# Nystrom attention with a mixture-of-experts layer on one core: a new order of the same work

## The chip, the cores and the metric

The kernel runs on one core of one Trainium2 chip. The metric is the device time of one execution in microseconds; several executions of the same kernel are timed and their median is given. A profile is one execution of its own.

## The reference, cut to what matters

Eight batches with eight heads of 576 positions and 64 channels go through Nystrom attention with 32 landmarks; the result, seen as 4608 tokens of 512 channels, goes through a top-1 layer of eight experts (512 to 1024 to 512).

```python
q_lm = q.reshape(B, H, m, S // m, D).mean(axis=3)          # k_lm likewise
A, Bm, C = sm(q, k_lm), sm(q_lm, k_lm), sm(q_lm, k)        # softmax of scaled products
Z = Bm.transpose(0, 1, 3, 2) / (norm1(Bm) * norminf(Bm) + 1e-06)
for _ in range(6):
    Z = 2 * Z - Z @ Bm @ Z
x = (A @ Z @ C @ v).transpose(0, 2, 1, 3).reshape(B * S, H * D)
xn = x / (norm(x) + 1e-06); en = expert_emb / (norm(expert_emb) + 1e-06)
logits = xn @ en.T / tau; expert_idx = argmax(logits)
probs = softmax(logits); gate_w = probs[arange(N), expert_idx]
out = gate_w[:, None] * (relu(x @ w1[expert_idx]) @ w2[expert_idx])
```

## The kernel before

The kernel works batch by batch and guesses, for each of the eight batches, one expert for all of its tokens (`guess`, `choose`); the guess is compared with the exact choice per token at the end, and a general path, which this input does not take, mends tokens that were guessed wrongly. So one batch b of attention is followed by one pair of expert layers: `first(b)` (W1, 512 to 1024, line 1469) and `second(b)` (W2, line 1498). The attention product with V is not written out; the product of the 32-row middle matrix and W1 (`first_weights`, `scaled`) makes a small weight `ww`, with which `first` multiplies the transposed softmax `ab` of the queries. Both expert layers work on 16-bit halves: a number is a high and a low half, and three products stand for one.

For each batch the attention side does this. `loads` and `load_values` bring K, Q and V. `sums` (lines 676 and 679) adds up 18 positions per landmark, partly by a POOL addition of halves and then a DVE reduction, partly by DVE alone. `inverse` and `powers` (to line 1020) make the 32x32 softmax matrix and its iterated inverse in tiny 32-bit products, each answered by a copy (`ek`, line 1016 on ACT or 1018 on DVE) and a DVE addition (line 1020). `values`, `peak`, `shifted`, `turned`, `weighted` make C and its product with V. `queries` and `scored` make A transposed (`ae`, `am`, `asum`, `at`, `ab`, lines 927 to 951). `landmarks` joins them into the small matrix `wt`. `rows`, `route` and `gates` make the exact logits and gates. On the weight side `weights` loads W1 and W2 of the guessed expert in four quarters each (the guess is read as a register, `gi`, line 1174); `first_scale` takes the sum of squares of W1 (four ACT steps, line 1346), `second_weights` the sum of absolute values of W2 (line 1425 on ACT or 1427 on DVE) and its two halves (lines 1450 to 1454). `hidden` makes the two halves of a hidden tile `ht` (ACT, line 1462, then DVE, line 1464, which frees the PSUM bank); `outputs` scales a chunk of results (line 1554 on DVE or 1556 on ACT) and sends it out.

All of these are Python generators that ask for one thing at a time: an operation on an engine, one of two engines for a movable copy (`"any"`), or a buffer or bank (`"get"`). The class `Weave` (line 165) holds them, and nothing in it decides anything: four tables written out in the file do. `TURNS` (line 56) is the sequence of generators to step, two base-36 digits for each, 2,705 steps in all. `CHOICES` (line 107) says for each movable copy which of its two engines takes it. `BANKS` (line 111) gives the first PSUM bank of each allocation. `WARM` (line 115) says before which turn how many units of 128 columns of idle products `keep_warm` (line 595) issues on PE, in matmuls of up to 512 columns into a bank that nobody reads. Each engine executes its instructions in the order in which the turns issue them, so the order across the engines is that of the table, held together by semaphores.

```python
            elif ask[1] == "pe":
                if turn in WARM:
                    warm(WARM[turn])
            self._step(n, got)
```

Of the kernel before, what the change touches and what calls it, by code (L numbers as in the profile page):

```python
# [53 lines left out]
BUFS = dict(k=2, q=2, v=2, ek=4, u=3, ec=2, ct=2, ae=3, at=2, st1=4, st2=4, w2=6, ww=2, ht=12, ab=3, yt=3, land=3, wt=3)  # L54

TURNS = (
    "060000060600330b000633060b330706073c0c3c0108000836000035013601013600013g0c013h0c34343g0101343j013h3401010c0134"
    "0134013k340101013734370134013m013f010i3o0h3j3o3j1i3m3l3o1j3f1i3n3o3o3j3n3m3o3m3f3o3k1i3o3n3o3j3o3l3k3k3o3k3o3i"
    "3n3f3m3o3l3o3n3o3o3o3o1i3o3i3m3o3l3m3f3o3f1k3o1i3n020h3m3s3o021i021k1i1i3m3m1k383838021l3n1l3n1k411j413n1k3n1k"
    "3r3m1k1k411j1k0d411l3m1k020d2n1k453n0e1l3m420e021j421j451j3q4247472m3q023n1j432m2m02384100451m4338383q38492m3n"  # L60
    "3q021j3q3s493s2m2m2m4a1m383q0i024a0i1m4e2m2m2m3q024c4c023q3q4i4d024d1m0n020n4g4j024e2m382m4h021m4f2m021m2m2m2m"
    "4g1m4f1m1n4t02382m4t4r2m1m024u4s021m2m1m2m4h38024s4i1m4u1m4i1m1n4w4w4v1m4y4i1n1o4y4i4y2m4y2m0i1m4x2m4r1n4v4x4z"
    "4z1m1m500o1m4y1m4f39391m2n1m50524f511n1m2n1m0t1n2n395251392n2n0o2n513t3t1p2m2n544y4y551p1o4y5557542n51551o0o0t"
    "572n3a1r1o4y2n533a3a1p2n532n0o532n2n1r4b533a1o4y552n2n3a2n2n5i3a2n3b553b543b3b3b2n1n2n4y1o2n2n5i2n4y555k1o2n5i"
    "1o2n555k1n5k2n5i5k5k031r5k035k1r03034b55034y032n2n2n2n034j2n035k5k2n544b4y031r032n035k4y4y551r2n1p1p5k034j4j4j"
# [24 lines left out]
    "05282bb805299v2v05050505052v052vao2vao052v052b0529282v2vap2v2b2vap9v0505052b2v2905b8ao2905059v052v2929bb2abb9i"  # L90
    "9v2b9ubbbabbbbbbbb29ba2b2v2v9u29akagb02vbcbdbd2v2b2va8ag4q2b2bbd2v2v2b2v2v2vbbbcbe2bbebc5fbb7v2vbb2vbb7v2b7v2b"
    "2vbb7vbbbf7vbb2v2v2w2bbb7w7w7w2w2v7w2bbb2v2v2vbbbfbbbe2v2v2vbb2v7w2b2b2bagagbb9k2b7ubhbhbhbbbi2bag9kbbbb1dbj9l"
    "2b9l9l2b2w2w2x2wbg1dbibj9lbm2wbl2wbi9lbibjbm9lblbp2w2wb1bjbq2wbp2wbpbrbp7xbgbp9l2wbr9lbubo2w2wbo3x1ebubu2w2xbu"
    "2xbubububsbvbt2w1e2wbt7x2wbs5f2wbybz2b2w2wbi2d2d7xbzbqc12dbi2w3b2wbi2wbjc27x2xbw2xbv2c2c2c2dc32d2dbw7x2cc37xc0"
    "c4c0c4c4c42xc2c12xb1byc4bic4b12x2xc6c7c7bi2xc4c4bic4c42xc82x2c2c2c2xbic62x2x2xbjbjcac82gc5bfc8cacacac5ca2x2x2g"
    "2cc4c82dc8b29lb22ebjc5c5c5bj2x9l9l2xc92xce2x2ebj9lbi2xc52x2e2g2x7xcecccbcbcbbib3cccc2x2ecb2x9mbj2dccb32xc93xb3"
    "b3cb2x2xbj2x2xb3ce9m2xb39m6hbj2g2x2g9m6h6hcj2g2e2e9n2g2xci2gci2g9n2e9n2e2e6hcj2g2x9ncj2x2g2x2x2ecjcj2g9n2g2xci"
    "b34q2g9n2f2gcbba9ob32x2g2x9lcncn2g2x2x2xcb2x9o2x2x2e9ockcn2gclclclcm9o2x2y2x2ycncc2ycccockcmcccn2y2ycp9ocpcm2y"
    "6h2y2gcn2y2y2y2y4qcucncrcr2i2i2z9o2y2ycc2yctcqcw2hcu2y2gctco2y2ycq2gcxcc2ycv2hcw2y2y2gb32y2hd0cv2h2zcc2y2gcy2i"
    "d22zcccx2ycbcycbd22hck2hc9csczd0d12y9oczd32gd42zd5d12zb32jcsd52h2hd42z4q2icsd39o2j2j2z2z2z2j2j5f2jcs2icb2z2z2z"  # L100
    "cb2zcb2i2z2l2z2l2z2z2z2z2z2l2zb32i2i2l2l2zcscscscs2l2j2jcs9icbcs2k2z2j2jcs2z2z2z2z2j2z2z2z2zdeda7x2z2z2z2zdade"
    "cccc2l2zdd2z2l2l2zdcdddd2zde7rda2zdcdcdbb32l2l2l30302zb42z2z2z2z2l2l2ldgb42zdg2zdf2l2l2zdfdfb42z2l2l2l2z3030b4"
    "b47x3030di302l3030dbdi30dmdkdbdmdldj3x2l30303030dk30dndo31do30302l303x30dpdldjdpdq3130dqdr30dn302l3030dvdt3131"
    "31dvds31dudrdudtdsdw31dw31317x31b53131313131b5b5b5b53131b6co3131b631b631b631b631dz31dh31b6b6b6b69odhdh31313131"
    "dzdzdz31319odzdz31313131dz31dz31dzb6dzdz32e031313131dx3131dydx31b031313132b3dydy3132e1e031dx3131e13131e03132e2"
    "e231313131e1e3e2e3e3")
CHOICES = (
    "01110100000001001010010010000000000000000000000010010010101000001010001101001001000001000110011101001110000000"
    "00000001000110000111110110001000000100100000000100110001000000000000001011001101001010101100100110010001001011"
    "010100100011111010100001100110")  # L110
BANKS = (
    "05150606460234605105507521370123476057614071230371567154135125251750567065467012417260450475047547107127024056"
    "75075074501651234761532604541316412371273101560510601504764750127501765212301276004465045710267106725430156035"
    "67301605017604750756730152654136712510042005705406575075654601234076521340762617156721340632061734074023")
# [50 lines left out]
class Weave:  # L165
# [55 lines left out]
    def run(self, turns, choices, banks, warm):  # L221
        choices, banks = iter(choices), iter(banks)
        for turn, n in enumerate(turns):
# [15 lines left out]
                if len(ask) > 6:  # L239
# [1414 lines left out]
```

## Time and profile before

| | us |
|---|---|
| median of 3 runs | 416.08 |
| lowest, highest of the runs | 413.51, 417.13 |
| the profiled execution | 416.43 |
| its span, first to last instruction | 414.7 |
| PE busy in the span | 393.4 |
| DVE busy | 338.0 |
| ACT busy | 237.2 |
| POOL busy | 77.8 |

The span is what the views of the profile are in; what lies around it (416.43 against 414.7) belongs to the launch. PE is the matrix engine, DVE the vector engine, ACT the scalar engine, POOL the general one, SP the engine that issues most DMAs. PE's busy time is modelled from pipelined products, so a busy PE is not PE at its peak.

### The profile page before, as it was taken

To read this page: it belongs to the slowest core of one execution; us is meant where nothing else is said; L and a number is where in the kernel's file an instruction comes from. 1 tells how busy PE (TensorE), PEld (TensorE's weight loads), DVE (VectorE), ACT (ScalarE), POOL (GpSimd) and SP (SyncE) were. 2 spreads that over 40 slices of the span, in tenths; PEclk is the share of its full clock that TensorE was granted. 3 is DMA by queue.
4 is the path that set the end of the run, shared out by engine and by line. 5 is a ranking of instruction groups with operands and counts; after the bars stand their busy time and mean duration, and the time that the engine had idled before them with its cause. 6 is when DMAs were issued, how large, how long until landed. Compare 5 with 4: busy or idle time off the path is not lost.

```text
span 414.7 us, 14529 instructions
## 1 busy us (share of the span) xinstructions
PE 393.4 (95%) x6078; PEld 242.3 (58%) x6078; DVE 338.0 (81%) x989; ACT 237.2 (57%) x530; POOL 77.8 (19%) x82
## 2 busy tenths in 40 slices
PE   4978999999999999999999998999999999999994
PEld 1445754577655774556755575456755585467644
DVE  5789998998798999968898899867899888777421
ACT  1267993475579757535748478635539657436310
POOL 5142146201220233202321241100302210000100
PEclk9699999999999999999999999999999999999999
DMA  8795793355596798052679067310492129231031
GB/s 312 298 363 240 275 351 127 118 189 192 159 380 220 240 320 310 36 195 71 237 269 382 32 172 308 115 36 17 130 339 103 63 57 346 114 133 39 3 140 60
DMA packets 23946, 77.68 MB, mean 187 GB/s; under 512 B 3008, under 2 KB 6336, under 8 KB 22080
## 3 DMA queue, kind: packets, MB, share of 16 engines
q1 hardware_dynamic: 23584, 76.49, 51.4%
q8 instruction: 49, 0.80, 0.8%
q10 hardware_dynamic: 288, 0.18, 0.2%
q14 instruction: 25, 0.20, 0.2%
HBM read 61.92 MB, written 14.75 MB: 185 GB/s over the span
## 4 chain that ended last, share of the span: by engine, by line
PE 62%; DVE 26%; ACT 5%; issue 3%; POOL 1%; DMA 1%; ACTq 0%; DVEq 0%
PE ps L513 60%; DVE ht L1464 4%; DVE w2c L1454 4%; DVE ksum L679 2%; DVE qsum L679 2%; POOL half L676 1%; DVE ae L927 1%; PE ps L599 1%; DVE ww L1411 1%; ACT ht L1462 1%; ACT junk L1217 1%; DVE asum L940 1%; DVE am L934 1%; DMA k_t<-kT 1%; ACT w2c L1452 1%
## 5 line engine op out<-in xcount | busy, mean ns | idle before, releaser
L513 PE MATMUL ps<-w2c,ht 128*128 128x512 f16 (+2 forms) x1176 | 197.2, 340 | 0.0
L513 PEld LDWEIGHTS <-ht 128*128 128x128 f16 (+1 forms) x1176 | 94.9, 102 | 81.0 <-issue 2.3
L513 PE MATMUL ps<-ab,ww 128*128 128x288 f16 x768 | 101.0, 286 | 1.9 <-DVE ht L1464 1.3
L513 PEld LDWEIGHTS <-ww 128*128 128x128 f16 x768 | 73.6, 98 | 26.0 <-issue 5.6
L1462 ACT ACTIVATE ht<-ps 128x288 f16<-128x288 f32 x128 | 47.4, 412 | 35.9 <-PE ps L513 35.3
L1464 DVE SCALAR_TENSOR_TENSOR ht<-ps,ht 128x288 f16<-128x288 f32 x128 | 54.0, 444 | 10.2 <-ACT ht L1462 9.6
L1454 DVE SCALAR_TENSOR_TENSOR w2c<-wstage,wsc,w2c 128x1024 f16<-128x1024 f32 x32 | 42.9, 1341 | 1.0 <-ACT w2c L1452 0.9
L1346 ACT ACTIVATE junk<-wstage 128x1024 bf16<-128x1024 f32 x32 | 33.9, 1060 | 0.7 <-DMA wstage<-w 0.3
L1217 ACT ACTIVATE junk<-ps 128x512 bf16<-128x512 f32 (+1 forms) x40 | 23.9, 596 | 15.0 <-DVE lg L1211 6.7
L1235 POOL TENSOR_TENSOR nrm<-ssq,half 128x5 f32<-128x5 f32 x8 | 10.3, 1283 | 111.3 <-ACT junk L1217 111.3
L1452 ACT ACTIVATE w2c<-wstage,wsc 128x1024 f16<-128x1024 f32 x23 | 26.2, 1148 | 6.5 <-DVE wsc L1436 6.3
L1556 ACT ACTIVATE yt<-ps,gfac 128x512 f32<-128x512 f32 (+1 forms) x24 | 15.0, 631 | 21.3 <-PE ps L513 15.8
L676 POOL TENSOR_TENSOR half<-q_t 128x576 f32<-128x576 f32 x13 | 17.9, 1376 | 46.2 <-DVE ksum L679 16.0
L961 POOL TENSOR_TENSOR ae<-ae,asum 128x576 f32<-128x576 f32 x13 | 15.2, 1166 | 59.0 <-DVE wgd L1118 19.0
L961 POOL TENSOR_TENSOR ae<-ae,am 128x576 f32<-128x576 f32 x14 | 16.6, 1192 | 42.6 <-DVE am L934 38.6
L676 POOL TENSOR_TENSOR half<-k_t 128x576 f32<-128x576 f32 x11 | 14.2, 1295 | 54.7 <-DMA k_t<-kT 24.6
L1411 DVE SCALAR_TENSOR_TENSOR ww<-ps,wsc,ww 128x1024 f16<-128x1024 f32 (+1 forms) x18 | 20.4, 1157 | 0.6 <-ACT ww L1409 0.6
L1409 ACT ACTIVATE ww<-ps,wsc 128x1024 f16<-128x1024 f32 (+1 forms) x18 | 17.5, 1016 | 5.7 <-PE ps L513 3.2
L1425 ACT ACTIVATE junk<-wstage 128x1024 bf16<-128x1024 f32 x18 | 18.9, 1050 | 0.2
L829 ACT ACTIVATE ec<-ps,cneg 128x576 f32<-128x576 f32 x16 | 11.8, 739 | 9.8 <-DVE cneg L823 7.5
L513 PE MATMUL ps<-ek 32*32 32x64 f32 (+1 forms) x768 | 16.0, 214 | 0.9 <-DVE ek L1020 0.7
L513 PEld LDWEIGHTS ps<-ek 32*32 32x32 f32 x768 | 11.5, 105 | 9.0 <-issue 4.2
(216 smaller groups left out, 528.2 us busy)
## 6 DMA issues: line engine op xcount, KB each, us to landing
wstage<-w SPq DMA_DIRECT2D x64, 512.0 KB, 6.7
v<-v SPq DMA_DIRECT2D x16, 512.0 KB, 5.3
k_t<-kT SPq DMA_DIRECT2D x7, 1152.0 KB, 7.9
q_t<-qT SPq DMA_DIRECT2D x7, 1152.0 KB, 7.1
out<-yt SPq DMA_DIRECT2D x31, 256.0 KB, 3.3
abs__137<-ab SPq DMA_DIRECT2D x8, 576.0 KB, 5.2
k_t<-kT SPq DMA_DIRECT2D x2, 576.0 KB, 4.3
q_t<-qT SPq DMA_DIRECT2D x2, 576.0 KB, 6.7
```

The lines of the kernel that those rows point to most:

```text
L513: pe.matmul(o, lhsT, rhs, start=start, stop=stop)
L676: pool.tensor_tensor(out=half, in0=sv[:, :, :, 0:9], in1=sv[:, :, :, 9:18], op=ALU.add)
L961: pool.tensor_tensor(out=x, in0=x, in1=z, op=op)
L1217: act.activation(junk[lo:hi, 0:512].rearrange("p (j g x) -> p j g x", j=4, g=2), pfv[lo:hi, :, n, :, 0:D], AF.Square, accum_out=ssq[lo:hi, ...
L1346: act.activation(junk, stage[1, b, q], AF.Square, accum_out=sq[:, q:q + 1])
L1409: act.activation(ww[:, 0], pw, AF.Copy, scale=sc)
L1411: vec.scalar_tensor_tensor(out=ww[:, 1], in0=pw, scalar=sc, in1=ww[:, 0], op0=ALU.mult, op1=ALU.subtract)
L1425: act.activation(junk, stage[2, b, q], AF.Abs, accum_out=sq[:, q:q + 1])
L1452: act.activation(w[:, 0], st, AF.Copy, scale=sc)
L1454: vec.scalar_tensor_tensor(out=w[:, 1], in0=st, scalar=sc, in1=w[:, 0], op0=ALU.mult, op1=ALU.subtract)
L1462: act.activation(ht[:, 0, r], ph[:, 0:HS], AF.Relu)
L1464: vec.scalar_tensor_tensor(out=ht[:, 1, r], in0=ph[:, 0:HS], scalar=0.0, in1=ht[:, 0, r], op0=ALU.max, op1=ALU.subtract)
```

## The change

All four tables are replaced; no other line differs. `TURNS` has the same 2,705 steps in another order. `CHOICES` moves copies: of the absolute sums of W2, ACT has 24 of 32 instead of 18; of the output scalings, 31 of 41 instead of 24; of the transposed scores' copies of 512 columns, 10 of 16 instead of 14; of the inverse's copies, 12 of 25 instead of 15; of the W2 halves, 24 of 32 instead of 23. POOL has 28 of 32 subtractions and multiplications of A instead of 27; its halves of the landmark sums stay at 24. `BANKS` gives other banks. `WARM` has twelve entries as before, 194 units in place of 153.

```diff
 TURNS = (
-    "060000060600330b000633060b330706073c0c3c0108000836000035013601013600013g0c013h0c34343g0101343j013h3401010c0134"
+    "060006060b0000060607063300330b3334340037000136070008010801003701010137353h01010c35013g35353h01013g01353j013i35"
...
 CHOICES = (
-    "01110100000001001010010010000000000000000000000010010010101000001010001101001001000001000110011101001110000000"
+    "01111000000011011100010000000000000000000000000000010100010000010000001010000001000110100000111010101110000000"
...
-WARM = {20: 38, 49: 19, 51: 6, 63: 5, 76: 2, 96: 12, 113: 8, 129: 17, 150: 17, 194: 20, 204: 2, 214: 7}
+WARM = {21: 77, 44: 20, 59: 4, 87: 8, 97: 12, 115: 8, 124: 7, 131: 19, 138: 1, 147: 18, 181: 18, 207: 2}
```

PE at the start, before: the end of the warming products in front of the first attention products (`ksum,qsum` is the inverse of batch 0, `k_t,qsum` its key products, `v_123` the column sums for its guess).

```order
L599 LDWEIGHTS ones_90
L599 MATMUL ps<-ones_90 128x512
L599 LDWEIGHTS ones_90
L599 MATMUL ps<-ones_90 128x256
L513 MATMUL ps<-ksum,qsum 32x32 x8
L513 MATMUL ps<-k_t,qsum 32x288 x16
L513 LDWEIGHTS v_123
```

The same place now:

```order
L599 LDWEIGHTS ones_90
L599 MATMUL ps<-ones_90 128x512
L599 LDWEIGHTS ones_90
L599 MATMUL ps<-ones_90 128x128
L513 MATMUL ps<-ksum,qsum 32x32 x8
L513 MATMUL ps<-k_t,qsum 32x288 x16
L513 LDWEIGHTS v_123
```

Of the matmuls of 512 columns, nine before and nineteen now, the last is shown; the attention products behind them stand as they did.

DVE about the guess of expert 0, before (`gm`, `g`, `ge`, `gi` are the guess, `nts`, `ntt`, `nm`, `cc`, `ccb` the norm for the inverse of batch 0):

```order
L1164 TENSOR_REDUCE gm<-ps 128x1
L748 TENSOR_REDUCE nts<-bt 128x2
L1167 TENSOR_SCALAR g<-ps,gm 128x8
L751 STREAM_TRANSPOSE ntt<-nts 128x64
L1170 SCALAR_TENSOR_TENSOR g<-g,iota 128x8
L754 TENSOR_REDUCE nm<-ntt 128x2
L757 TENSOR_SCALAR cc<-nm 128x1
L759 RECIPROCAL cc<-cc 128x1
L1172 TENSOR_REDUCE ge<-g 128x1
L762 COPY ccb<-cc 128x32
L1174 CAST gi<-ge 128x1
```

The same place now:

```order
L1164 TENSOR_REDUCE gm<-ps 128x1
L748 TENSOR_REDUCE nts<-bt 128x2
L1167 TENSOR_SCALAR g<-ps,gm 128x8
L1170 SCALAR_TENSOR_TENSOR g<-g,iota 128x8
L751 STREAM_TRANSPOSE ntt<-nts 128x64
L1172 TENSOR_REDUCE ge<-g 128x1
L1174 CAST gi<-ge 128x1
L754 TENSOR_REDUCE nm<-ntt 128x2
L757 TENSOR_SCALAR cc<-nm 128x1
L759 RECIPROCAL cc<-cc 128x1
L762 COPY ccb<-cc 128x32
```

The cast of the guess, for which the weight loads wait, has moved ahead of `nm`, `cc` twice and `ccb`.

ACT up to the first scaled weights, before (`ct` are copies of transposed scores, `ek` copies of the inverse, `ae` the exponentials of A, `junk,wsq<-wstage` the sums of squares of W1, `be` the exponential for the inverse of batch 1, `ww` the scaled weights):

```order
L882 COPY ct<-ps 128x512
L1016 COPY ek<-ps 128x64
L885 COPY ct<-ps 128x128
L937 ACTIVATE ae<-ae 128x576 x2
L1016 COPY ek<-ps 128x64
L1346 ACTIVATE junk,wsq<-wstage 128x1024 x3
L714 ACTIVATE be<-be 128x64
L1346 ACTIVATE junk,wsq<-wstage 128x1024
```

The same place now:

```order
L882 COPY ct<-ps 128x512
L937 ACTIVATE ae<-ae 128x576
L885 COPY ct<-ps 128x128
L1346 ACTIVATE junk,wsq<-wstage 128x1024
L937 ACTIVATE ae<-ae 128x576
L1346 ACTIVATE junk,wsq<-wstage 128x1024 x3
L714 ACTIVATE be<-be 128x64
```

Two copies of the inverse have left ACT for DVE, one square sum stands before the second exponential of A, and the exponential for batch 1 has moved behind the last square sum.

## Rows read from the trace of the kernel before

**Rows 1.** The page: busy times of the engines, and PE's clock in 40 slices.

```profile
PE 393.4 (95%) x6078; PEld 242.3 (58%) x6078; DVE 338.0 (81%) x989; ACT 237.2 (57%) x530; POOL 77.8 (19%) x82
...
PEclk9699999999999999999999999999999999999999
```

**Rows 2.** Stretches: length, busy PE, PEld, DVE, ACT, POOL, PE clock, DMA share, GB/s.

```profile
10.86:18.35 7.49, 7.40 (x110) 3.45 (x117) 5.58 (x33) 1.81 (x5) 0.00 (x0) 0.54 0.84 337
18.35:34.66 16.31, 13.87 (x351) 8.28 (x336) 14.35 (x44) 10.28 (x22) 7.15 (x6) 1.00 0.95 343
...
52.57:405.60 353.03, 347.43 (x5329) 213.85 (x5320) 293.72 (x835) 207.88 (x467) 62.55 (x50) 1.00 0.49 174
```

**Rows 3.** Timeline of PE, 0 to 20 us: start, length, what, [idle before].

```profile
5.15 3.67 PE L599 MATMUL ps<-ones 128*128 128x512 bf16 x10
9.48 0.27 PE L513 MATMUL ps<-ksum,qsum 64*32 64x32 f32 x8 [0.66 <-DVE qsum L679]
...
10.94 1.59 PE L513 MATMUL ps<-k_t,qsum 64*32 64x288 f32 x28
...
13.34 2.19 PE L599 MATMUL ps<-ones 128*128 128x512 bf16 x5
...
17.35 1.66 PE L513 MATMUL ps<-q_t,ksum 64*32 64x288 f32 x32
```

**Rows 4.** Stretches of the warming products alone (line 599): busy PE and PEld, clock.

```profile
5.15:8.10 2.95, 2.95 (x7) 1.04 (x8) 1.00 1.03 416
8.10:8.90 0.80, 0.72 (x4) 0.20 (x2) 1.00 1.00 410
...
32.90:34.05 1.15, 1.09 (x5) 0.41 (x5) 1.00 1.11 437
```

**Rows 5.** Timeline of DVE, 8 to 39 us.

```profile
8.07 2.73 DVE L679 TENSOR_REDUCE qsum<-q_t 128x64 f32<-128x1152 f32 x2
...
15.79 0.17 DVE L1164 TENSOR_REDUCE gm<-ps 128x1 f32<-128x8 f32 x1 [0.97 <-PE ps L513]
...
17.20 0.14 DVE L1174 CAST gi<-ge 128x1 int32<-128x1 f32 x1
...
18.65 0.78 DVE L927 STREAM_TRANSPOSE ae<-ps 128x576 f32<-128x576 f32 x1 [0.52 <-PE ps L513]
...
28.85 0.23 DVE L708 TENSOR_REDUCE bm<-ps 128x2 f32<-128x64 f32 x1 [0.61 <-PE ps L513]
...
30.22 0.29 DVE L1071 COPY wt<-ps 128x128 f32<-128x128 f32 x1 [0.88 <-PE ps L513]
...
38.34 0.23 DVE L1111 TENSOR_SCALAR wen<-ps,scw 128x16 f32<-128x16 f32 x1 [0.79 <-PE ps L513]
```

**Rows 6.** Timeline of PE, 32 to 40 us.

```profile
32.96 1.25 PE L599 MATMUL ps<-ones 128*128 128x512 bf16 x5
...
34.66 1.05 PE L513 MATMUL ps<-ab,ww 128*128 128x288 f16 x6
...
39.12 1.20 PE L513 MATMUL ps<-k_t,qsum 64*32 64x288 f32 x32
```

**Rows 7.** Groups by line: busy us, mean ns | idle before, releaser.

```profile
L1464 DVE SCALAR_TENSOR_TENSOR ht<-ps,ht 128x288 f16<-128x288 f32 x128 | 54.0, 444 | 10.2 <-ACT ht L1462 9.6
...
L1554 DVE TENSOR_SCALAR yt<-ps,gfac 128x512 f32<-128x512 f32 (+1 forms) x17 | 11.5, 678 | 5.0 <-PE ps L513 4.2 <-DVE misi L1582 0.8
...
L1427 DVE TENSOR_REDUCE wsq<-wstage 128x1 f32<-128x1024 f32 x14 | 16.6, 1202 | 0.0
...
L1425 ACT ACTIVATE junk<-wstage 128x1024 bf16<-128x1024 f32 x18 | 18.9, 1050 | 0.2
...
L1556 ACT ACTIVATE yt<-ps,gfac 128x512 f32<-128x512 f32 (+1 forms) x24 | 15.0, 631 | 21.3 <-PE ps L513 15.8 <-DMA out<-yt 2.6 <-issue 1.8
```

**Rows 8.** Timeline of all engines, the last 10 us.

```profile
405.61 3.76 PE L513 MATMUL ps<-w2c,ht 128*128 128x256 f16 x33
...
409.96 0.36 ACTq L1561 DMA_DIRECT2D out<-yt  x1
```

More of the change, by code (lines that the diff above doesn't have):

```diff
@@ new lines @@
+    "350135353801011i0c0c3k010c0138010i3f1i1i013f013o3n3o3j3k3o3o1i1i3o3m3j3o1i1i1i3f3n3j3i3k3j3n3o3o3i3k0h3i3o3m3k"
+    "3o3i3o3o3f3o1k3l3o0d3n3o3n3o3o3f3l3o3o3m3o3o3m3o3k1k3f0d023k1j023o3n02393k393k1k1k3n023k3n0h1j391l3n1k1l0e3x0n"
+    "43431k1j1k1l1l3k0e1k431k3k1k021k3v4446443n46473n3n3k44472m433w45002m1j39392m434602452m1j490n1j3v1m392n394a3v3v"
+    "2m491m023n3x1j3x02024a022m3v1m2m021j4j023v4l3v2m2m0i0i394j3v024k024o4m2m4k3v02021m4q2m024l1n2m2m0i2m024n2m2m1m"
+    "391m4m1m2m4n1m2m024p4u1m4u1m4t021m4r394t4v024p4v1m2m2m1m1m390o4y4z4o4y4x4z0t1m4x4o2m1m4w2m4o2m4o4x4x4r4w1m4n4x"
@@ new lines @@
+    "503a501m1m1m3a4n512n1m1m4x4s2n1m1n3a2n2n2n1m3a2n52510t1p1n3y524x1n4x3y0o1p1o5c4i1o2n1o4s4s5c5b1n2n2m0o5f5b4s1o"
+    "5f1r2n5d0o4x5c3b3b5d5d2n2n3b2n3b3b2n2n4x3b1n1o5c1o5d2n5c5h1r5b1o5h2n3c3c3c2n4x2n5h2n2n2n3c2n2n4x1n1r1o2n2n3c2n"
+    "4q5h5c5c035j034x5j1r4x031p5j2n035b4x5j03034q1r5j2n2n1r4i5j4x4q2n5j5j5c03035j4q035j1n2n2n032n2n5c5b1r5b2n4x4i03"
+    "4x5j1p4i4i03031p4x035i4x035b4x2n5i5l1p5g4x5b03030j4i5g4x1p5l3z1p1r035c3z3z5b03030j032n5b03393z2n2n3z3z035b5i1r"
+    "5b1p5q2n035q5q5r5l5q5r1r361r5q5c3z1q1r0k1p5r3z5c2n1p5s5t1r5r5r5b5c4c2n2n2n2n2n5r5s3z2n5p2n5r2n5s5t5r5t5r4c1r4c"
@@ new lines @@
+    "1r3z5u5u2o5r5p2p0k1r5r5r5w2o2o1r2o2o5x2o5z0u5w2o5x645z633z2o2o1r65615r3z635v63626261665r2o1r5u5r662o1r5r5v672o"
+    "63632o2o646569645r1r60675r5v6860645r5r645v541r5v5p5r685v402p0z5r5r4e4e2p2p0u4e69400p4e40405g4b2o1r4e4e1r2o6d3z"
+    "2p6d0z6d6d406b6c6c416d41414e2p2p4e6l6l2o0p6l416l6l2o2o2o4e6l6l1s416o6p6o4d6q4d3w6m1s2o6b1t2o6p6r1s6q2o4e6r6s42"
+    "0q1s6m6q2o6r6s1t6t6q426u6q421u6t1s1s6u5454422p1t6y2p6x0q6r2p2p2p422p0u716x2p6q6q6y2p2p6q4e6b53716q2p721s2p1s2p"
+    "6r7372736q7372716r2p713c716q6r712p71712p710u71722p1u716q6r6r723c6w2p2p6q1t4e736w706w2p2p1u2p6r74731u6r6r1w6w70"
@@ new lines @@
+    "6w4f742p1w1t1t2p6w562p2p2p4f2p564f794f79561t1t6r4g1w2p561u6e2p4g1w56562p742p1u4g1w1w1u2p4g0v7a757a1u4g1w7a1w1u"
+    "1w2p1u1w104g1w2p1u1v7a7a107e7c4h4b1w2p1w7b7b7b0v7d561w792p2p2p2p7c2p4h2p4h2p562p4h7d7g7g4h757c7d2q2q2r557g1w7g"
+    "551w2q7k102q2q0w7k0w7l7l1w7g2q2q2q2q1w2q7p7g7p7m7h7g757n101x1w7r2q1x1y2q7n7r2q2q7q7k7e1y2q7t7m421w1x7j2q7e7t7u"
+    "7q2q7s7l2q7v1x2q151x7h2q1x7y7i2q7x7j2q2r7v2r1w7y1w6f1x1y1w802q2q1x7x817z2r2r7w7i7s7s817u827z7w7s827k2r7l801w2r"
+    "1z1y1y1z1z2r7i6f6f041y04567i887k2r2r7i7i2r7l2r7h047i880456877i2r2r2r2r04217l1y04048a7i2r87047l708b041z7k7k2r16"
@@ L107 @@
+    "302ldhdhdf312l3030dkdia3dg30a3dl30302l30dfdn3030302ldj2ldodn31dj30dldodmdm30306k3030dt2l30dkdpdp3030dsdqdrdqdu"
+    "dsdw3131dhdr313131dvdtdudvdw313131ao31aoao3131ao313131ao313131dfapapaj31313131apap31ap31apapapa3ap31dzamdzdzdz"
+    "3131dzdzdzdzdz3131codzdz3142e03131313131313131dxe0e0ap3132dy313132dy31dy31dx3131313231313131323131e231e131e131"
+    "e2a03131dxe3e3e3e1e2")
 CHOICES = (
-    "01110100000001001010010010000000000000000000000010010010101000001010001101001001000001000110011101001110000000"
```

84 lines of the change are left out of this document (30 added, 54 removed).

## The prediction

> **What bounds the kernel now.** I began with the page's busy times and slices [rows 1]: PE is busy 393.4 of 414.7 us, and its clock is at full speed in every slice but the second, which stands at 6 tenths. So the question is where PE stands still or runs slowly, since the multiplications themselves are the same before and after. The view by stretches [rows 2] answers it. I cut the span at the end of the first landmark sums (10.86 us), at the end of the half-speed stretch (18.35), at the first expert product (34.66) and at 52.57, where the second layer of expert 0 begins. From 52.57 to 405.6 us PE is busy 347.43 of 353.03 us: only 5.60 us are idle in 353. That long middle is bound by PE, and an order of work can win 5.60 us there at most.
>
> The start is different. From 10.86 to 34.66 us PE does little expert work; it serves a chain (landmark sums, the small inverse, softmax, first-layer weights) that mostly runs on DVE. DVE is busy 5.58 of 7.49 us in the first part and 14.35 of 16.31 in the second [rows 2]: it is idle for 1.91 + 1.96 = 3.87 us in all. PE's granted clock is 0.54 in the first part, 1.00 in the second. [...]
>
> Where that clock comes from is seen in the timeline of PE [rows 3]. Ten warming products run from 5.15 to 8.82 us, then little stands in PE's row until DVE ends the sums at 10.80 [rows 5]. The first seven of the ten take 2.95 us, 0.42 each, though the view shows 1.00 there (the records of the clock begin later); the last three, two and a half in columns, take 0.72 with the tail of the last [rows 4]. Five of 512 columns at full speed take 1.09 us, 0.218 each [rows 4]. So PE reached full pace at about 8.1 us, then rested, and fell to half in the stretch that begins at 10.86.
>
> **The change, part by part.** *The start.* In front of the first attention product 77 units of 128 columns now stand in place of 38, twenty products in place of ten. Seven at 2.95 us together bring PE to 8.1 us as before; the other thirteen (12 of 512 columns and one of 128) at 0.218 us for 512 need 12.25 × 0.218 = 2.7 us and end at 10.8. The product behind them waits for the sums that DVE ends at 10.8. So the 39 added units (about 2.1 us) lie wholly beside DVE's sums and cost nothing; if the clock did not rise at 8.1 they would end near 5.15 + 19.25 × 0.42 = 13.2 us, 2.4 us late.
>
> With no idle time before 10.86 I expect the full clock from there on. Rows at half and at full clock give the price: the products of keys with landmark queries take 1.59 us, partly still at full speed [rows 3], against 1.20 us for such a set at full speed [rows 6]; the warming two steps behind them takes 2.19 us for 19 units [rows 3] against 1.25 us for 20 [rows 6]. That is 1.33 us of PE time less ahead of the product for the guess of expert 0, and the query products behind it (1.66 us, [rows 3]) shrink to 1.20.
>
> What this is worth is read from DVE, which works in between. Two of its waits in this stretch end by PE: 0.97 us before the guess and 0.52 us before the transposed scores [rows 5]. Most of both goes; DVE's own order up to the guess leaves PE ready first. I take 1.4 us of these 1.49. The guess also comes first in DVE's new row, ahead of four small steps of the inverse that stood before it, so the weight loads are issued about a microsecond sooner, and on ACT the exponential of batch 1 now stands behind the four square sums rather than before the last. In the second stretch DVE waited 0.61 us for the product of batch 1's landmarks and 0.88 us for the first product with the inverse [rows 5]. Both come through five warming products, which are still there (18 units in place of 17), and earlier sums put the first one sooner; I take half of 1.49, 0.7 us. Two copies of the inverse move from ACT to DVE ahead of the first expert product, and two steps as small move behind it: +0.1 us. The start thus gives 1.4 + 0.7 − 0.1 = 2.0 us, between 0 (DVE's other waits take their place) and 3.87 (DVE never idle).
>
> *Behind the first expert product.* There DVE waited 0.79 us for the gating product [rows 5], which stood behind two warming products. One short warming product and an expert product that is needed anyway stand there now, and the copy before them moves from DVE to ACT. I take 0.5 us, between 0 and 0.79.
>
> *The middle.* Stages come in the same succession: each expert's two layers hold the same attention work between them to within a few products. The movable copies shift load: seven output scalings (0.678 us on DVE, 0.631 on ACT) and six absolute sums of second-layer weights (1.202 on DVE, 1.050 on ACT) go from DVE to ACT [rows 7]; four copies of transposed scores go the other way, and the rest is smaller. So DVE loses 7 × 0.678 + 6 × 1.202 = 12.0 us in these and gets some 3 back, and ACT gains 7 × 0.631 + 6 × 1.050 = 10.7 us. DVE is the busier (293.7 of 353.0 us against ACT's 207.9, [rows 2]), so this leans to the good. But nearly all of these copies lie beside PE's work already. For the waits that a new order makes or removes the trace of before has no row; the bounds are 5.60 us gained (no idle left) and 10.7 us lost (all that ACT gains ends up in front of PE). I take 0: idle places of the same kind, elsewhere.
>
> *The tail.* From 405.61 us the last products, a last scaling and an output DMA from ACT at 409.96 end the span [rows 8]. The products of expert 7's second layer follow each other as before; I take 0, with 0.4 us either way for an output that is issued sooner or later.
>
> **The sum.** The profiled execution took 416.43 us for a span of 414.7: 1.73 lie around it. 414.7 − 2.0 − 0.5 = 412.2 us of span, 413.9 with what lies around it. The profiled execution lies 0.35 above the median of the runs (416.08), so against that median it is 413.6 us.
>
> [...] PE held the full clock from 18.35 to 34.66 us though it was idle for 2.44 of 16.31 us in many small pieces [rows 2], and lost it behind the 2 us from 8.82 to 10.86, in which one small set of products ran for 0.27 us [rows 3]. [...]
>
> **The rivals.** *B, the middle gains as well.* DVE, the busier of the two helpers, is relieved by some 9 us net, and 4 of the 5.60 us of idle time go. For it: DVE is busy 83% of the middle. Against it: idle time there also comes from long chains, which relief does not shorten. 413.6 − 4.0 = 409.6 us.
> *C, the start gives nothing.* The clock falls all the same, or the longer warming ends late by up to 2.4 us, or DVE meets other waits. For it: the clock is half in the trace whenever PE had rested, and the moment at which it rises is not fixed by the program. Against it: twenty products leave no rest. Both gains gone: 416.1 us.
> *D, the other side.* ACT work that came over from DVE stands in ACT's queue ahead of the first step of a hidden tile. DVE already waited 9.6 us for that ACT step in all [rows 7], and PE's next product waits for the bank that DVE frees. Its places are the first layers beside which sums moved, above all that of expert 7, whose four sums were all on DVE and of which three are now on ACT; a sum of 1.05 us there delays PE by what the free banks do not cover. All of it would be 10.7 us; it turns the result to slower from 2.5 of these on (23%). With two thirds, 413.6 + 7.1 = 420.7 us. Against it: ACT is busy only 59% of the middle.
>
> **How the numbers follow.** The forecast has 0.45, B 0.25, C 0.12, D 0.18. A measurement of this kernel can tell about 1% (4.2 us) from no change: under 411.9 or over 420.2 us. Nearly all of B (0.22) and a fifth of the forecast's own case (0.08) fall below: 0.30 faster. Two thirds of D lie above: 0.12 slower. The rest, 0.58, is within 1%. The range runs from 408.5 (B with its last microsecond) to 418.5 us (D at under half its price); the forecast's own range is 411.5 to 415.5.
>
> **What would show it.** Right: the second slice at full clock; twenty warming products that end by about 10.8 us; the guess of expert 0 cast some 1.3 us sooner than 17.20 [rows 5]; the first expert product at about 32.6 us in place of 34.66 [rows 6]; DVE idle for under 2 us from 10.86 to there; about 5 to 6 us of idle PE in the middle; the last DMA from ACT about 2.5 us sooner. Wrong: a granted clock at half anywhere between 11 and 18 us; warming products still running at 12 us; the first expert product later than 34 us; more than 9 us of idle PE between it and the last product, or waits of PE that ACT's absolute sums or output scalings end.

## The result and the profile after

The changed kernel takes 412.37 us in the median of 20 executions (409.38 to 415.90), the kernel before 415.77 (413.51 to 417.81): 3.4 us less; ratio 0.9907, 95% interval 0.9887 to 0.9928. The ratios in this text are estimated from the single executions, without the few in a slower state, and are not quotients of the medians. A second series gave 412.87 us, ratio 0.9921 (0.9886 to 0.9957). The forecast was 413.6, the range 408.5 to 418.5. The number was close; the reasons were not.

The profiled execution of the changed kernel is the fastest of its 20: 409.38 us, span 407.6, 1.78 around it. The profiles differ by 7.1 us of span where the medians differ by 3.4, so no sum over the two profiles can be the result; they are read by stretches. The page of the changed kernel (answers to [rows 1]):

```profile
PE 392.8 (96%) x6087; PEld 243.2 (60%) x6087; DVE 324.9 (80%) x979; ACT 246.1 (60%) x544; POOL 79.7 (20%) x83
...
PEclk9999999999999999999999999999999999999998
```

The second slice is at full clock now; DVE is 13.1 us less busy, ACT 8.9 us more. The stretches that answer to [rows 2] (length, then busy PE, PEld, DVE, ACT, POOL, clock):

```profile
11.40:18.35 6.95, 6.16 (x143) 3.12 (x142) 5.83 (x32) 1.81 (x5) 0.00 (x0) 1.00 0.85 336
18.35:32.93 14.58, 13.88 (x314) 8.04 (x315) 14.01 (x43) 9.79 (x20) 7.11 (x6) 1.00 0.98 353
32.93:50.32 17.39, 16.16 (x265) 11.59 (x262) 16.60 (x61) 16.07 (x37) 2.59 (x2) 1.00 0.75 281
50.32:398.63 348.31, 346.01 (x5329) 214.51 (x5320) 282.22 (x828) 215.95 (x481) 64.45 (x51) 1.00 0.49 175
```

The first expert product stands at 32.93 (34.66 before, [rows 6]): 1.73 us less. From there to the second layer of expert 0 it is 17.39 us (52.57 − 34.66 = 17.91 before): 0.52 less. The last stretch holds the same 5329 matmuls as the one of [rows 2] and is 348.31 us long in place of 353.03: 4.72 less, with 2.30 us of idle PE in place of 5.60 and 1.42 us less busy time. What I had set at nothing gave most. The timeline of PE at the start (answers to [rows 3]):

```profile
5.20 6.27 PE L599 MATMUL ps<-ones 128*128 128x512 bf16 x20
11.40 0.27 PE L513 MATMUL ps<-ksum,qsum 64*32 64x32 f32 x13
...
13.14 1.24 PE L599 MATMUL ps<-ones 128*128 128x512 bf16 x5
```

And that of DVE (answers to [rows 5]):

```profile
8.05 2.60 DVE L679 TENSOR_REDUCE qsum<-q_t 128x64 f32<-128x1152 f32 x2
11.80 0.22 DVE L708 TENSOR_REDUCE bm<-ps 128x2 f32<-128x64 f32 x1 [0.60 <-PE ps L513]
...
15.28 0.17 DVE L1164 TENSOR_REDUCE gm<-ps 128x1 f32<-128x8 f32 x1 [0.17 <-PE ps L513]
16.14 0.15 DVE L1174 CAST gi<-ge 128x1 int32<-128x1 f32 x1
17.84 0.78 DVE L927 STREAM_TRANSPOSE ae<-ps 128x576 f32<-128x576 f32 x1
...
27.07 0.23 DVE L708 TENSOR_REDUCE bm<-ps 128x2 f32<-128x64 f32 x1 [0.42 <-PE ps L513]
28.71 0.29 DVE L1071 COPY wt<-ps 128x128 f32<-128x128 f32 x1
```

The reader is to see two things. The waits of 0.97, 0.52 and 0.88 us are nearly gone and the guess is cast 1.06 us sooner (forecast: some 1.3). But the sums end at 10.65 and the twenty warming products at 11.47, and a new wait of 0.60 us stands on the first row behind them. One execution is one draw here; the experiments show others.

The tail: the last DMA from ACT is issued at 402.99 (409.96 in [rows 8]) and only follows the stretches above: from the end of the last of them to the end of the span it is 8.97 us (414.7 − 405.60 = 9.10 before).

### The profile page after: what moved, and what is told of

Its sections match the earlier page's. It is cut to its first block, busy times and chain, and to the rows that moved or that the text cites. A ratio compares the mean times of both kernels' runs of the same rounds, so it can differ in the third digit from the quotient of the medians.

```text
span 407.6 us, 14587 instructions
## 1 busy us (share of the span) xinstructions
PE 392.8 (96%) x6087; PEld 243.2 (60%) x6087; DVE 324.9 (80%) x979; ACT 246.1 (60%) x544; POOL 79.7 (20%) x83
## 4 chain that ended last, share of the span: by engine, by line
PE 86%; DVE 9%; ACT 1%; issue 1%; DMA 1%; ACTq 0%; DVEq 0%
PE ps L513 82%; PE ps L599 2%; DVE w2c L1454 2%; DVE ht L1464 2%; PE ps L877 1%; DMA con<-emb 1%; DVE cm L821 1%; ACT ww L1409 0%; ACT junk L1217 0%; DVE ksum L679 0%; PE ps L878 0%; DVE ww L1411 0%; DVE at L946 0%; DVE asum L940 0%; DVE lg L1243 0%
## 5 line engine op out<-in xcount | busy, mean ns | idle before, releaser
L1346 ACT ACTIVATE junk<-wstage 128x1024 bf16<-128x1024 f32 x32 | 33.8, 1058 | 0.4
L1235 POOL TENSOR_TENSOR nrm<-ssq,half 128x5 f32<-128x5 f32 x8 | 9.4, 1174 | 119.9 <-ACT junk L1217 119.9
L1556 ACT ACTIVATE yt<-ps,gfac 128x512 f32<-128x512 f32 (+1 forms) x31 | 19.1, 628 | 16.5 <-PE ps L513 9.3
L961 POOL TENSOR_TENSOR ae<-ae,asum 128x576 f32<-128x576 f32 x14 | 16.4, 1171 | 60.5 <-DVE asum L790 28.3
L1452 ACT ACTIVATE w2c<-wstage,wsc 128x1024 f16<-128x1024 f32 x24 | 27.6, 1155 | 0.0
L676 POOL TENSOR_TENSOR half<-k_t 128x576 f32<-128x576 f32 x11 | 15.3, 1392 | 59.1 <-DMA k_t<-kT 26.4
L1425 ACT ACTIVATE junk<-wstage 128x1024 bf16<-128x1024 f32 x24 | 25.4, 1057 | 1.3 <-DMA wstage<-w 1.1
L676 POOL TENSOR_TENSOR half<-q_t 128x576 f32<-128x576 f32 x13 | 18.9, 1450 | 35.2 <-DMA q_t<-qT 18.6
L949 ACT ACTIVATE ab<-at 128x576 f16<-128x576 f32 x16 | 10.9, 682 | 13.7 <-DVE at L946 13.7
```

The source lines that it names most:

```text
L676: pool.tensor_tensor(out=half, in0=sv[:, :, :, 0:9], in1=sv[:, :, :, 9:18], op=ALU.add)
L961: pool.tensor_tensor(out=x, in0=x, in1=z, op=op)
L1346: act.activation(junk, stage[1, b, q], AF.Square, accum_out=sq[:, q:q + 1])
L1425: act.activation(junk, stage[2, b, q], AF.Abs, accum_out=sq[:, q:q + 1])
L1452: act.activation(w[:, 0], st, AF.Copy, scale=sc)
L1556: act.activation(yt[:, 0:n], py[:, 0:n], AF.Copy, scale=fac)
```

## The experiments

The medians of the kernel before were 415.88, 415.59 and 415.37 us in the three series below.

**The start of one, the rest of the other.** Order, choices and warming of one kernel up to the first expert product, of the other from there on (the first 204 or 198 steps of `TURNS`):

```diff
-WARM = {21: 77, 44: 20, 59: 4, 87: 8, 97: 12, 115: 8, 124: 7, 131: 19, 138: 1, 147: 18, 181: 18, 207: 2}
+WARM = {20: 38, 49: 19, 51: 6, 63: 5, 76: 2, 96: 12, 113: 8, 129: 17, 150: 17, 194: 20, 213: 2}
 TURNS = (
-    "060006060b0000060607063300330b3334340037000136070008010801003701010137353h01010c35013g35353h01013g01353j013i35"
+    "060000060600330b000633060b330706073c0c3c0108000836000035013601013600013g0c013h0c34343g0101343j013h3401010c0134"
...
```

> Order, movable copies and warming products of the kernel before up to the first expert product; from there on those of the changed kernel. The changed kernel had 412.4 us in the median, the one before 415.8. Theory 1 (the gain is the start: clock kept, waits of DVE gone, 2 us): about 414.4 to 415.4 us, the clock at half from about 11 to 18 us, the first expert product at about 34.7 us as in rows 6. Theory 2 (the gain comes from the order behind the first expert product, fewer idle pieces of PE in the middle): about 412.4 us, with 2 to 3 us of idle PE from the second layer of expert 0 to the end, in place of 5.60. Rival (the two profiled executions differ by chance in the middle): idle PE there of 5 us or more although the order is that of the changed kernel.

Measured: 409.63 us (408.98 to 413.18), ratio 0.9844 (0.9802 to 0.9885), 2.7 us faster than the changed kernel itself. Its profile kept the full clock (mean 1.0) with the start of before, and the first expert product stands at 32.97, as in the changed kernel (32.93). So the 1.73 us between the first two profiles go with the fall of the clock in one execution: without it the start of before is as soon.

> Order, movable copies and warming products of the changed kernel up to the first expert product; from there on those of the kernel before. Theory 1 (the start is worth 2 us): about 413.4 to 413.8 us, full clock from about 9 us on, first expert product at about 32.9 us, idle PE in the middle near the 5.60 us of rows 2. Theory 2 (the order behind it is what counts): 415 to 415.8 us though the first expert product is sooner, the time given back before the end. If both parts count and add, this kernel's gain and that of its counterpart sum to 3.4 us.

Measured: 417.81 us (415.77 to 421.25), ratio 1.0037 (1.0010 to 1.0064), 1.9 us slower than the kernel before. So neither theory as I had it: the rest of the change wins some 6 us, and its start, in which I had seen the whole gain, loses 2 to 3. Put in alone the two parts give −6.2 and +1.9 us, −4.3 together, where the whole change gives −3.4: they add up to within 1 us. The rest from the second layer of expert 0 to the last product, in the kernel before, the changed one, the first of these two and the second:

```profile
52.57:409.37 356.80, 351.20 (x5362) 216.99 (x5352) 295.19 (x839) 207.88 (x467) 62.55 (x50) 1.00 0.49 173
```

```profile
50.32:402.40 352.08, 349.78 (x5362) 217.65 (x5352) 282.22 (x828) 216.70 (x482) 64.45 (x51) 1.00 0.50 175
```

```profile
50.39:402.38 351.99, 349.72 (x5362) 217.89 (x5352) 282.76 (x828) 216.74 (x482) 63.35 (x51) 1.00 0.50 174
```

```profile
52.64:409.57 356.93, 350.89 (x5362) 217.03 (x5352) 294.53 (x839) 207.70 (x467) 62.55 (x50) 1.00 0.49 173
```

With the same order this part takes the same time to 0.15 us in these four, whatever came before it; over all ten profiles of one of the two orders with its own choices it takes 356.8 to 357.2 us in the old one and 351.7 to 352.7 in the new. So 4.8 us belong to the order and choices of the rest, and the rival of a chance difference falls. The medians give the rest more than that, 6.2; what makes up the difference is not shown (falls of the clock, treated below, come in about half of the executions of the kernel before and in one of six here).

**The first warming alone.** Only the number of units in front of the first attention product differs: 38 in the changed kernel, 77 in the kernel before, 77 and none in the kernel of 409.6 us.

```diff
-WARM = {21: 77, 44: 20, 59: 4, 87: 8, 97: 12, 115: 8, 124: 7, 131: 19, 138: 1, 147: 18, 181: 18, 207: 2}
+WARM = {21: 38, 44: 20, 59: 4, 87: 8, 97: 12, 115: 8, 124: 7, 131: 19, 138: 1, 147: 18, 181: 18, 207: 2}
```

> The changed kernel with 38 units of warming in front of the first attention product, as before, in place of 77; nothing else. If the longer warming is what keeps the clock (the prediction): the granted clock falls to half from about 11 us, DVE again waits 0.5 to 1 us before the guess, the first expert product stands 1.0 to 1.5 us later than 32.9, and the time is 413.4 to 413.9 us. Rival (the start gains by the order of the guess and the weight loads alone, the clock does not matter): 412.4 us or, since the long warming ended 0.6 us late, 411.8 us, first expert product at or before 32.9 us.

Measured: 410.61 us (409.93 to 411.81), ratio 0.9856 (0.9823 to 0.9889): 1.8 us faster than with 77. Better than the rival had it, and with the clock kept: the mean granted clock is over 0.995 in five of the six executions (0.999 in the profiled one).

> The kernel before with 77 units of warming in front of the first attention product in place of 38; nothing else. If the clock alone gives the start's gain: full clock from about 9 us, the waits of 0.97 and 0.52 us of rows 5 mostly gone, the first expert product at about 33.3 us, 414.3 us. If the order of the guess and the weight loads is needed as well: the waits go but the first expert product moves by under 0.5 us, 415.3 to 415.8 us. If the warming ends late (by 0.6 us in the changed kernel): 415.8 to 416.4 us.

Measured: 416.42 us (414.52 to 418.87), ratio 1.0003 (0.9975 to 1.0032): nothing gained, as the case of a late end had it.

> The kernel that had 409.6 us (order of before up to the first expert product, that of the changed kernel behind it), now with 77 units of warming in front of the first attention product in place of its 38. Taking the 39 units off the changed kernel won 1.8 us, adding them to the kernel before lost 0 to 0.6. Theory (the longer warming ends late by an amount that depends on when the clock rises in an execution): 410.5 to 411.5 us, a wide spread of executions (over 4 us), and the first attention product later than the end of the sums by 0.3 to 1.5 us. Rival (the 39 units cost nothing, the loss in the changed kernel came with its order at the start): 409.4 to 410 us.

Measured: 413.20 us (410.66 to 416.56), ratio 0.9929 (0.9893 to 0.9965): 3.6 us lost, more than the theory asked, with the wide spread that it did ask. The late end is not all of it: DVE waits only 0.49 us for it in this profile, but the clock is at half (0.50) from 30 to 36 us and the first expert product stands at 36.98. The mean granted clock is 0.995 or less in 7 of the 12 executions, against one of six with 38 units.

> The kernel that had 409.6 us, without any warming in front of the first attention product (0 units in place of 38; 77 gave 413.2). Theory (warming there is needed for the clock, only not so long): PE runs at half clock far into the first 20 us, the first expert product later than 34 us, 411 to 413 us. Rival (the clock rises by the attention products themselves soon enough): 409 to 410 us.

Measured: 410.66 us (409.57 to 413.79), ratio 0.9871 (0.9821 to 0.9921): by the medians 1.0 us is lost against 38 units (the intervals overlap: not clear of noise) and 2.5 are won against 77. Its theory had the kind right and the price too high. Five warming products at 14.45 take 1.94 us in its trace, where they take 2.19 at half clock [rows 3] and 1.24 at full clock in the changed kernel; the two at 16.37 take 0.49, full pace. So PE was slow to about 16 us, though the view shows 1.00 there (in the traces of the kernel before and of the changed one the records of the clock begin at 8.11 and 9.17 us, and the view shows 1.00 ahead of them), and the first expert product stands at 34.09. Even so this start is cheaper than 77 units.

> The changed kernel once more, beside the two above. It had 412.4 us (409.4 to 415.9). If the longer warming costs by how late it ends, the spread of executions is again over 4 us and the median 411.8 to 413; in the trace the end of the twenty warming products stands behind the end of the sums by 0.3 to 1.6 us.

Measured: 412.87 us (410.56 to 416.02), ratio 0.9921 (0.9886 to 0.9957), as expected of a late end. The profiled execution, at 415.13 us, lies 2.3 us above this median and shows what the first profile hid. Timelines of DVE and PE and one stretch:

```profile
5.03 1.24 DVE L606 TENSOR_TENSOR e<-con 64x64 f32<-64x64 f32 x1 [2.50 <-DMA con<-emb]
...
13.47 0.22 DVE L708 TENSOR_REDUCE bm<-ps 128x2 f32<-128x64 f32 x1 [1.16 <-PE ps L513]
```

```profile
7.01 6.14 PE L599 MATMUL ps<-ones 128*128 128x512 bf16 x20
```

```profile
38.00:45.40 7.40, 6.62 (x81) 3.34 (x81) 5.24 (x20) 4.50 (x11) 1.50 (x1) 0.54 0.53 219
```

The warming begins behind a small product of the embeddings, and that behind `e`, a DVE step that waits for their DMA. Here `e` ended at 6.27, not 4.47, the warming ran from 7.01 to 13.15, and DVE, through with the sums at 11.77 and with three small steps at 12.31, waited 1.16 us. And the clock fell all the same, at 38 us. In the seven profiled executions with 77 units DVE always waited on that row: 0.25, 0.44, 0.49, 0.60, 1.16, 1.43 and 1.52 us; in the six with 38 units never. So 39 units more cost 0.8 us there on average, where I had worked out nothing. The 1.16 came from a late begin; the two longest come from a late rise of the clock. In the kernel with 1.43 us (417.81, above) the twenty products began at 5.76 and took 7.11 us, against 6.27 and 6.14 in the two profiles of the changed kernel. In that with 1.52 us (the changed order with the copies of before, further down) the warming began at 5.27, and its first fourteen products still took 0.42 us each. The stretch of warming products alone, then DVE's row:

```profile
5.27:11.17 5.90, 5.90 (x14) 2.11 (x15) 1.00 1.03 406
```

```profile
12.80 0.22 DVE L708 TENSOR_REDUCE bm<-ps 128x2 f32<-128x64 f32 x1 [1.52 <-PE ps L513]
```

In the changed kernel with 38 units `e` was as late as in this second profile (4.91 and 5.03) and the sums ended at 11.64 and 11.77; the first expert product stands at 33.62 there and at 35.38 here.

> A second look at the kernel with the changed start and the order of before behind it: in nine of its twelve executions the mean granted clock was 0.995 or less, which costs 1 to 3 us, but not in the one that was profiled; in the changed kernel one of twenty was that low. If the fall lies at the start (half clock somewhere before 33 us), the start of the changed kernel does not guard against it; if it lies behind the first expert product, where the order of before leaves PE idle for 1.13 us at 36.8, it belongs to the order of the rest.

Measured: 416.77 us (one execution; of the twelve, ten and not nine were at 0.995 or less). The fall lay at the start: half clock from about 29 to 33 us (0.50 from 30 to 32), in front of the first expert product, though the warming had been 77 units.

What is left of the start is its order. The changed kernel with 38 units and the kernel of 409.6 us have the same warming, the same sums (end at 11.64 and 11.65) and full clock; the first expert product stands at 33.62 in the one and 32.97 in the other. DVE in the changed order:

```profile
16.44 0.15 DVE L1174 CAST gi<-ge 128x1 int32<-128x1 f32 x1
...
17.76 0.25 DVE L770 SCALAR_TENSOR_TENSOR ek<-ps,rct,ident 128x32 f32<-128x32 f32 x1
...
27.90 0.21 DVE L1020 TENSOR_TENSOR ek<-ek,ps 128x64 f32<-128x64 f32 x1
29.40 0.29 DVE L1071 COPY wt<-ps 128x128 f32<-128x128 f32 x1
```

and in the order of before:

```profile
16.76 0.15 DVE L1174 CAST gi<-ge 128x1 int32<-128x1 f32 x1
17.23 0.25 DVE L770 SCALAR_TENSOR_TENSOR ek<-ps,rct,ident 128x32 f32<-128x32 f32 x1
...
26.93 0.16 DVE L1020 TENSOR_TENSOR ek<-ek,ps 128x64 f32<-128x64 f32 x1
28.64 0.29 DVE L1071 COPY wt<-ps 128x128 f32<-128x128 f32 x1 [0.89 <-PE ps L513]
```

The guess comes 0.32 us sooner, but the first step of the inverse 0.53 later (0.23 of it stand already in front of the guess: `gm` begins at 15.58 and 15.35), its fourth 0.67 (23.65 and 22.98) and its last 0.97 later. PE's queue, in which a product waits for each step, is 0.68 late behind the fourth (23.92 and 23.24) and 0.65 at the first expert product. The last step is not what holds `wt`: it ends 0.55 and 1.09 us before PE, behind five warming products, begins the product that `wt` copies (28.66 and 28.18). Which part of the order makes the inverse late was not tested. The sooner guess made the weights early (the sums of squares end on ACT at 27.6 in place of 29.0), which nobody waited for.

**Choices alone, order alone.** The engines of 40 movable copies (output scalings, sums and halves of W2) exchanged between the kernels; order, warming, banks and all other copies kept. So "the order" is here the order with its banks and the other copies; the banks were never exchanged by themselves. In the kernel before:

```diff
-    "00000001000110000111110110001000000100100000000100110001000000000000001011001101001010101100100110010001001011"
+    "00000000000100000101110110001000000100000000000010100001010000000010111001001100001000011101100100000001101001"
...
```

> The kernel before in its own order, with the 40 movable copies of output scalings, sums of W2 and halves of W2 on the engines that the changed kernel gives them; nothing else. So far the order and choices behind the first expert product gained about 5 to 6 us together. If the relief of DVE by these copies is what gains (rival B as the prediction put it): 411 to 413 us, the two waits of PE for DVE's hidden step at 206.6 and 255.4 (0.81 and 0.52 us in the kernel before) gone. If the order gains: 415 to 416.5 us, the same waits in the same places. Rival D (ACT's new work stands in front of hidden steps): over 417 us.

Measured: 420.25 us (418.66 to 423.78), ratio 1.0105 (1.0071 to 1.0139): 4.7 us slower, in the range of rival D. The relief of DVE did not end PE's longest wait for its hidden step: 0.80 us at 204.58 (0.81 at 206.58 before); that at 255.44 shrank from 0.52 to 0.29.

> The counterpart: the changed kernel with those 40 copies on the engines of the kernel before. If the choices gain: 414.5 us or more (2 us or more lost against 412.4). If the order alone gains: 412 to 413 us, DVE about 12 us busier, idle PE in the middle still 2 to 3 us.

Measured: 416.50 us (412.76 to 417.79), ratio 0.9998 (0.9962 to 1.0033): 4.1 us slower than the changed kernel, in the range of choices that gain. The same long stretch in these two:

```profile
50.50:413.11 362.61, 353.91 (x5360) 217.88 (x5352) 281.80 (x825) 218.82 (x487) 62.48 (x50) 1.00 0.48 170
```

```profile
52.37:409.15 356.78, 351.25 (x5361) 218.28 (x5352) 294.17 (x842) 205.37 (x462) 63.77 (x51) 1.00 0.49 172
```

The order alone gives 356.78 us, as much as before (356.80). The choices alone give 362.61, though DVE is 13.4 us less busy. Only both give 352.08. DVE, PE and one stretch of the kernel with the choices alone:

```profile
287.20 1.28 DVE L1454 SCALAR_TENSOR_TENSOR w2c<-wstage,wsc,w2c 128x1024 f16<-128x1024 f32 x1 [4.16 <-ACT w2c L1452]
```

```profile
291.28 0.43 PE L513 MATMUL ps<-u,ek 32*32 32x64 f32 x16 [1.44 <-DVE ek L1020]
```

```profile
290.00:295.00 5.00, 3.72 (x32) 2.56 (x33) 4.08 (x8) 1.09 (x4) 1.14 (x1) 0.69 0.65 184
```

A first half of W2 had gone from DVE to ACT, where it stands behind steps that wait for other results; DVE's next step needs it and holds its whole queue for 4.16 us, an inverse step among it; PE waits 1.44 us for that, and the mean clock is 0.69 from 290 to 295 us. One copy put back:

```diff
-    "00000000000100000101110110001000000100000000000010100001010000000010111001001100001000011101100100000001101001"
+    "00000000000100000101110110001000000100000000000010100001010000000010111001001100001000111101100100000001101001"
```

> The kernel with the order of before and the changed kernel's choices (420.25 us), with one single copy put back to DVE: the first half of the second quarter of expert 5's W2. In that kernel's trace DVE stood 4.16 us (283.0 to 287.2) in front of its second half, because ACT reached the first half only behind five other steps; PE's wait of 1.44 us at 291.28 and a clock of 0.69 from 290 to 295 followed. Theory (an order written for one set of choices loses by other choices at a few places where one engine's queue waits for the other): 416.5 to 418 us, the 4.16 us wait gone. Rival (ACT is simply loaded too much, in many places): 419.5 to 420.3 us.

Measured: 417.53 us (415.55 to 420.49), ratio 1.0042 (1.0009 to 1.0075). One copy of 40 gives back 2.7 of the 4.7 us, as the theory had it; from 283.71 to 298.72 PE is busy throughout. The other 2.0 us were not traced to single copies.

**The order in one stretch.** From the second layer of expert 2 to the first layer of expert 5 the tables of the changed kernel, else those of before (steps 1067 to 1927).

```diff
-    "802q2q7j1y1y80831x7z847i2q827j7y1x83847j1w2q2r852r1y2q1x871y86821x881w2r2q882r1x7z8382871w1y898986811z6c811y2r"
+    "802q2q7j1y1y80831x7z847i2q827j7y1x83847j1w2q6b1x1x852r2r851w6c1x1y1w872q2q1x88862r2r818282887z89868182892r7k87"
...
```

> The kernel before, except that from the second layer of expert 2 to the first layer of expert 5 (about 153 to 283 us) the order, choices and banks of the changed kernel stand. In the kernel before, PE's waits of 0.5 us and more in that stretch are six with 4.37 us together (184.3 to 259.3); in the changed kernel three with 1.58. Theory (the gain of the middle is these waits): 412 to 413.5 us, the other 1 to 2 us of the gain lying before 153 us. Rival (the gain is spread evenly from 35 to 400 us): 414 to 414.5 us. Rival (what is won here is given back at the next seam): 415.5 us or more.

Measured: 413.05 us (411.21 to 414.32), ratio 0.9925 (0.9889 to 0.9961): 2.5 us by the medians, as the theory had it. From the second layer of expert 0 to the last product this kernel takes 353.47 us, 3.3 less than before: most of the 4.8, from a third of the length. The same 2018 matmuls in the kernel before and in this one:

```profile
152.82:282.98 130.16, 125.65 (x2018) 74.75 (x2016) 112.75 (x321) 78.94 (x175) 25.49 (x21) 1.00 0.51 181
```

```profile
151.61:278.43 126.82, 125.04 (x2018) 75.12 (x2016) 107.57 (x322) 80.92 (x177) 25.16 (x20) 1.00 0.53 184
```

3.34 us less, 2.73 of them idle PE. The waits of PE that went are these of the kernel before, all six:

```profile
184.33 0.28 PE L513 MATMUL ps<-wgd,ab 32*128 32x72 f16 x13 [1.01 <-issue]
192.39 1.20 PE L513 MATMUL ps<-q_t,ksum 64*32 64x288 f32 x32 [0.50 <-ACT junk L1217]
206.58 0.90 PE L513 MATMUL ps<-ab,ww 128*128 128x288 f16 x6 [0.81 <-DVE ht L1464]
216.52 0.43 PE L513 MATMUL ps<-u,ek 32*32 32x64 f32 x16 [0.85 <-DVE u L863]
255.44 0.90 PE L513 MATMUL ps<-ab,ww 128*128 128x288 f16 x6 [0.52 <-DVE ht L1464]
259.29 0.66 PE L877 MATMUL ps<-ident,ec 128*128 128x128 f32 x4 [0.68 <-DVE ht L1464]
```

Four of the six (2.86 of 4.37 us) end by DVE, three of them by a hidden tile's second half. Those of the changed kernel in the same stretch:

```profile
193.38 0.36 PE L513 MATMUL ps<-gr,ones 128*128 128x8 f32 x2 [0.63 <-DVE gr L1159]
239.23 6.14 PE L513 MATMUL ps<-ab,ww 128*128 128x288 f16 x48 [0.68 <-DVE ht L1464]
253.16 6.42 PE L513 MATMUL ps<-w2c,ht 128*128 128x512 f16 x29 [0.27 <-DVE w2c L1454]
```

Nothing of the gain is given back at the seam: behind it both kernels take 126.39 us.

## Why the prediction was right in its number and wrong in its reasons

*The start, −2.0 us: wrong in sign.* Against the order of before the changed start costs 1.9 us (kernel before) or 2.7 us (kernel of 409.6 us). The step that failed is "the 39 added units lie wholly beside DVE's sums and cost nothing". It took one execution's moment of the clock's rise, 8.1 us, as given. It was 9.2 in the changed kernel's profile and some 11.1 in that of the kernel with 1.52 us, and the begin of the warming moved between 5.1 and 7.0 us. The 2.4 us of rival C for an end that is late by all of it was the better half of the working: the price came out at 0.25 to 1.52 us in seven traces and at 1.8 us in the medians of the changed kernel with 77 and 38 units. The other 1.0 us (410.61 − 409.63) would be the order; six executions each do not set it clear of noise, but the two profiles with the same sums show 0.65. I counted the inverse steps that the guess passes as a gain for the guess and set nothing against it for the inverse, whose steps now come later.

*"With no idle time before 10.86 I expect the full clock from there on": wrong.* The clock fell in front of the first expert product or shortly behind it in executions with 0, 38 and with 77 units (0.50 over the middle of each fall, 0.57 in one of them), at 11 to 18, 14 to 17, 24 to 28, 29 to 33, 30 to 36, 36 to 43 and 38 to 45 us. It needed no rest of 2 us, as I had read it from one execution: the longest pause of PE just ahead of these falls was 1.58 us (at 27.98 in the kernel of 413.2 us). By the mean granted clock of each execution (0.995 or less) it fell in 38 of 79 executions of the kernel before, with a median of 417.3 us against 415.0 in the others, and in 4 of 32 of the changed kernel; these counts are low, for five profiled executions at 0.996 hold a short fall too. So the 1.4 us that I put on the clock is a price that only about half of the executions of before pay. That the changed kernel pays it less often is real, but not by its 77 units: with the same start and the order of before behind it the clock was that low in 10 of 12. Nor is it the rest's order alone: with the start of before and 77 units ahead of that order it was 7 of 12. What guards it stays open.

*The 0.7 us in the second stretch and the 0.5 us behind the first expert product.* The waits shrank as worked out (0.88 gone, 0.61 to 0.42; that for the gating product 0.79 to 0.51, the stage behind the first product 0.52 us shorter). The first went under in the late inverse. The second is not shown: at full clock that stage took 17.14 to 18.17 us in seven profiles with the order of before and 17.22 to 17.90 in four with the new one.

*The middle, 0: wrong.* "Idle places of the same kind, elsewhere" was a guess without a row. The gain was 4.7 us, of which the idle time that I had set as the bound holds 3.3; the rest is busy time of PE that shrank, 1.42 us, so 5.60 was no true bound; why it shrank is not shown. Rival B had the place and the size (4 of 5.60), but not the way: the relief of DVE alone loses 5.8 us in that stretch and the order alone wins nothing. Rival D's direction was right for the choices without their order, but the place that a run settles is not a hidden tile's first step: there a moved copy itself came late on ACT, and DVE's queue stood for it. With the order that came with them, waits of that size are gone from PE's row. I priced order and choices as two terms; the two exchanges show them as one.

*The tail, 0: right.* The second layer of expert 7 takes 24.42 us in both.

The sum: −2.0 − 0.5 + 0 was written; the runs show about −6.2 for the rest (with the first stage behind the seam) and +2.7 for the start on top of it. That 413.6 and 412.4 are neighbours is luck: two errors of opposite sign. The kernel with the start of before and the rest of the change, 409.63 us, beats both.

## What to carry to other kernels

Warming products cost nothing only where they end before the work behind them in every execution: do not size them from the start and the rise of the clock in one profile; here 77 units ended late in seven profiles of seven, 38 in none of six. An order written out by hand and the choice of engine for each copy are one design; judge neither by the load of an engine, and test them exchanged. Where two errors can cancel, exchange the halves of a change before believing a forecast that came true.

## What the runs showed of the hardware that was not expected

*A small DVE step that ended with POOL's addition.* `e`, two inputs of 64x64, took 0.22 us in ten profiled executions and 1.23 or 1.24 us in four: in those it began at 4.91 to 5.03, 0.11 or 0.12 us behind POOL's addition of halves (4.79 to 4.92, 1.27 or 1.28 us long), and ended 0.07 or 0.08 us behind its end. In three of the ten (the kernel before, the changed one, and the kernel before with 77 units) the addition began at 4.77, 4.82 and 5.06, 0.35 us or more behind the end of `e`. That the addition held `e` up is my reading of these times; no run tests it. In the two profiles of the changed kernel `e` waited 1.72 and 2.50 us for the DMA of the embeddings, the addition 1.52 and 1.61 us for that of K: which of the two came first went by those DMAs. Between these two profiles `e` began 0.78 us later and took 1.02 longer; that moved the begin of the warming by 1.8 us (5.20 to 7.01) and the sums behind `e` on DVE by 1.1 (8.05 to 9.17).

*The rise of the clock.* The warming that began at 5.15 reached full pace at 8.1 us, that from 5.20 at 9.2, that from 5.27 at some 11.1: 2.95, 4.0 and some 5.8 us behind the first warming product. What sets the moment is not shown. The stage behind the first expert product took 20.65 us with a fall in it (second profile of the changed kernel, mean clock 0.83) and 17.39 without (the first, 1.00).
